# A fused attention and gated feed-forward kernel: x of batch 1 on the GpSimd DMA queue, and another order of the loading phase

## The chip, the core and the metric

The kernel runs on one NeuronCore of a Trainium2 chip. The metric is the device time of one execution in microseconds, as the median of several runs; smaller is better. Five engines work side by side, each through its own list of instructions in order: TensorE (PE in the profile, its weight loads PEld), VectorE (DVE), ScalarE (ACT), GpSimd (POOL) and SyncE (SP), which here only starts DMA transfers. ACT and POOL start transfers too. Transfers that SP starts appear in the profile as queue q1, those of ACT as q10 and those of POOL as q0; all of them are carried by the same 16 DMA engines. Engines wait for each other and for transfers by semaphores.

## What is computed

Eight batches of x (8 heads, 512 tokens, 64 channels) meet a small state (8 heads, 32 rows). Both directions of attention between them are computed, joined to 544 rows of 512 per batch, and put through a feed-forward layer with a sigmoid gate.

```python
scores = scale * np.matmul(x, state.transpose(0, 1, 3, 2))
a = np.exp(scores - scores.max(-1, keepdims=True))
a /= a.sum(-1, keepdims=True) + 1e-09
xread = np.matmul(a, state)
scores2 = scale * np.matmul(state, x.transpose(0, 1, 3, 2))
a2 = np.exp(scores2 - scores2.max(-1, keepdims=True))
a2 /= a2.sum(-1, keepdims=True) + 1e-09
sread = np.matmul(a2, x)
x = np.concatenate([xread, sread], axis=2)   # to (4352, 512)
gate = 1.0 / (1.0 + np.exp(-(x @ w_gate)))
return (gate * (x @ w_val)) @ w_out
```

x, the state and the weights (512 by 1536, 512 by 1536, 1536 by 512) are given as float32, and so is the result.

## The kernel before

The matrix products run in bfloat16. Weights and most of the state are turned into bfloat16 by POOL's transfers themselves; x arrives as float32 (`xf`) and is cast on an engine into `xb` (`cast_x`). A batch then goes through these steps:

- x is transposed to `xT`: for batches 0 and 1 on PE with copies by ACT or DVE (`xT_mm`, `xT_cp`, and `xT_mm2`, `xT_cp2`, two head pairs at a time), for later ones by four transposing transfers on SP (`at_xT_dma`).
- `S_mm` multiplies `xT` with the padded state `sTz`, `S_exp` takes the exponential on ACT. `n_sum`, `n_mul` (or `n_sums`, `n_muls`) on DVE normalise over the state rows into `ab`; `aT_mm` and `aT_cp` (or `aT_dma`) transpose that to `aT`.
- `at_Eb`, `p_tok` and `p_fold` on POOL prepare the other direction, `sr_mm` and `sr_fin` finish it into `XS`, a ninth "batch" that holds the 256 state rows of all batches.
- The attention output isn't formed for the tokens. Instead `sw_visit` (or `sw_wide`) multiplies the state with the weights, and `sw_cp` copies the result to `SW`. For each block f of 128 hidden columns (12 of them), `gv_mm` multiplies `SW` with `aT` and so gives the gate and value projections; `gv_th` (tanh on ACT) and `gv_glu` (DVE) join them into `glu`.
- `out_mm` multiplies four blocks of `glu` with a piece of `wo`; three of these make 128 rows of output, which ACT copies out and SP stores.

PSUM is divided into two banks for `gv`, one for `outp`, four for `swp` and one for `at`; a step names its bank (`GV`, `OU`, `SWP`, `AT`) and waits until what last stood there has been read.

There is no scheduler: the program order of each engine is the order in which the calls are written. From L424 to L673 stands a list of calls, written out one by one, the loading phase. In it x, the weights and the state arrive, batches 0 and 1 are projected, batch 0 is multiplied with `wo`, and batch 2 is prepared. The first call of the loop over b (L675) makes `SW` of batch 3; from there each turn projects batch b, multiplies batch b-1 with `wo` and prepares batch b+1.

Loads of the list, before: SP loads x of batches 0 and 1 in four pieces each (two heads, 256 KB a piece, `load_x(.., 4)`). ACT loads the first quarter of the state (`load_s`), POOL the three others (`load_sb`), the gate and value weights in pieces of 256 or 512 columns (`load_w`; w=0 is `wg`, w=1 is `wv`), `wo` in three pieces (`load_wo`), and x of batches 2 and 3. A POOL transfer is issued by an instruction in POOL's own list and so waits for whatever stands ahead of it. `gate` is a tiny POOL copy out of a tile that a transfer fills: it holds back all that follows on POOL until that has landed. `warm` runs small matmuls on constants, 68 in all.

Of the kernel before, what the change touches and what calls it, by code (L numbers as in the profile page):

```python
# [8 lines left out]
FP = mybir.dt.float32  # L9
BF = mybir.dt.bfloat16  # L10
# [6 lines left out]
def kernel(  # L17
# [14 lines left out]
    nc = tc.nc  # L32
# [55 lines left out]
    def cast_x(b, cp, lo, n):  # L88
        if b not in xbs:
            xbs[b] = xp.tile((128, 4, H, D), BF, name="xb")  # L90
        cp(xbs[b].rearrange("p c h d -> p h c d")[:, lo:lo + n], xfs[b][:, lo:lo + n])  # L91
# [358 lines left out]
    sT_mm(0, SWP)  # L450
    xT_cp(0, 0, vec)
    warm(20, OU)
    cast_x(0, act, 2, 2)
    cast_x(0, vec, 6, 2)
    xT_mm(0, 1, SWP)
    sT_pad(0, 0, vec)
    sT_pad(0, 1, act)
    S_mm(0, 0, SWP, (0,))
    xT_cp(0, 1, vec)
    xT_mm(0, 2, OU)  # L460
    cast_x(1, vec, 2, 2)
    cast_x(1, pool, 0, 2)
    xT_mm(0, 3, GV)
    load_w(1, 1024, 512)
    xT_cp(0, 2, act)
    cast_x(1, pool, 6, 2)
    xT_cp(0, 3, vec)
    cast_x(1, vec, 4, 2)
    load_w(0, 0, 256)
    load_sb(3)  # L470
    S_mm(0, 0, AT, (1,))
    S_exp(0, 0)
    S_mm(0, 1, AT, (0,))
    xT_mm2(1, 0, OU)
    S_mm(0, 1, OU, (1,))
    S_exp(0, 1)
    warm(12, AT)
    xT_cp2(1, 0, act)
    n_sum(0, 0)
    xT_mm2(1, 1, SWP)  # L480
    S_mm(1, 0, GV)
    n_sum(0, 1)
    xT_cp2(1, 1, vec)
    S_mm(1, 1, SWP)
    S_exp(1, 0)
    at_Eb(0)
    sw_visit(0, 256, 256)
    n_mul(0, 0, nc.vector)
    n_mul(0, 1, nc.vector)
    S_exp(1, 1)  # L490
    sT_mm(1, GV)
    sw_cp(0, 256, 2, 1, act)
    p_tok(1)
    n_sums(1)
    sw_cp(0, 256, 2, 0, act)
    aT_mm(0, GV)
    sT_cp(1, act)
    aT_cp(0, 0, act)
    sr_mm(0, AT)
    sw_visit(1, 256, 256)  # L500
    sw_visit(0, 1024, 512, 0)
    aT_cp(0, 1, vec)
    n_muls(1, nc.vector)
    load_sb(2)
    gv_mm(0, 3, GV)
    sw_cp(1, 256, 2, 0, act)
    sw_cp(1, 256, 2, 1, act)
    gv_th(0, 3)
    load_w(1, 0, 256)
    aT_mm(1, OU)  # L510
    sw_cp(0, 1024, 0, 1, act)
    sw_visit(1, 1024, 512, 0)
    sw_cp(0, 1024, 0, 0, vec)
    gv_glu(0, 3)
    sw_cp(1, 1024, 0, 1, act)
    sw_visit(0, 1024, 512, 1)
    sw_cp(1, 1024, 0, 0, vec)
    sw_cp(0, 1024, 1, 0, act)
    sw_visit(1, 1024, 512, 1)
    sw_cp(0, 1024, 1, 1, vec)  # L520
    gv_mm(0, 11, GV)
    aT_cp(1, None, vec)
    sw_cp(1, 1024, 1, 0, act)
    gv_mm(0, 2, SWP)
    sw_cp(1, 1024, 1, 1, act)
    load_w(0, 512, 512)
    gv_th(0, 2)
    gv_th(0, 11)
    gv_mm(1, 2, SWP)
    sr_fin(0)  # L530
    gv_glu(0, 2)
    gv_th(1, 2)
    load_x(2, nc.gpsimd)
    gv_mm(0, 9, SWP)
    gv_glu(0, 11)
    gv_mm(1, 8, GV)
    gv_th(0, 9)
    gv_th(1, 8)
    sT_mm(3, OU)
    gv_glu(1, 2)  # L540
    sw_visit(1, 0, 256)
    gv_glu(0, 9)
    load_w(1, 512, 512)
    sw_visit(0, 0, 256)
    gv_glu(1, 8)
    sw_cp(1, 0, 2, 1, act)
    gv_mm(0, 8, GV)
    sT_mm(2, AT)
    sw_cp(1, 0, 2, 0, act)
    sw_visit(0, 512, 512, 0)  # L550
    sw_cp(0, 0, 2, 0, vec)
    gv_th(0, 8)
    sw_cp(0, 0, 2, 1, vec)
    sT_cp(2, act)
    gv_glu(0, 8)
    sT_cp(3, act)
    sw_visit(1, 512, 512, 0)
    gv_mm(1, 11, GV)
    load_wo(0)
    sw_cp(0, 512, 0, 0, act)  # L560
    sw_cp(0, 512, 0, 1, vec)
    gv_th(1, 11)
    gv_mm(0, 0, SWP)
    gv_glu(1, 11)
    gv_mm(1, 9, GV)
    sw_cp(1, 512, 0, 1, act)
    at_Eb(1)
    sw_cp(1, 512, 0, 0, act)
    gv_th(1, 9)
    gv_th(0, 0)  # L570
    cast_x(2, vec, 4, 4)
    p_fold(1)
    gv_glu(1, 9)
    gv_mm(0, 1, SWP)
    gv_mm(0, 10, GV)
    gv_th(0, 1)
    gv_glu(0, 0)
    gv_th(0, 10)
    sr_mm(1, AT)
    gv_glu(0, 1)  # L580
    gate(xfs[0][:, 7, 0, 0:1])
    cast_x(2, pool, 0, 4)
    sw_visit(0, 512, 512, 1)
    gv_glu(0, 10)
    sw_visit(1, 512, 512, 1)
    sw_cp(0, 512, 1, 0, vec)
    sw_cp(0, 512, 1, 1, act)
    gv_mm(1, 0, GV)
# [8 lines left out]
    gv_glu(1, 0)
    gv_glu(0, 5)
    sr_fin(1)
    gv_mm(0, 6, SWP)  # L600
    gv_mm(0, 7, GV)
    gv_mm(0, 4, SWP)
    gv_th(0, 6)
    gv_th(0, 7)
    out_mm(0, 1, OU)
    gv_glu(0, 6)
    gv_th(0, 4)
    S_mm(2, 1, SWP)
    gv_mm(1, 4, SWP)
    S_mm(2, 0, GV)  # L610
    gv_glu(0, 4)
    gv_glu(0, 7)
    out_mm(0, 7, SWP)
    S_exp(2, 1)
    S_exp(2, 0)
    gv_mm(1, 6, GV)
    gv_th(1, 4)
    gv_th(1, 6)
    out_mm(0, 0, AT)
    gv_glu(1, 6)  # L620
    gv_mm(1, 7, GV)
    gv_glu(1, 4)
# [6 lines left out]
    out_mm(0, 3)
    n_add(2)  # L630
    gv_glu(1, 7)
    n_muls(2, nc.vector)
    out_mm(0, 9)
    at_Eb(2)
    aT_dma(2)
    p_fold(2)
    out_mm(0, 4)
    gv_th(1, 3)
    gv_glu(1, 3)
    out_mm(0, 5)  # L640
    out_mm(0, 11)
    gv_mm(1, 1, GV)
    gv_th(1, 1)
    sw_wide(2, 0)
    out_mm(0, 6, GV)
    gv_glu(1, 1)
    sw_cp(2, 0, 0, 1, act)
    sw_cp(2, 0, 1, 0, act)
    sr_mm(2, GV)
    sw_cp(2, 0, 1, 1, act)  # L650
    sw_cp(2, 0, 2, 1, act)
    sw_cp(2, 0, 0, 0, vec)
    out_mm(0, 8)
    cast_x(3, pool, 0, 4)
    sw_cp(2, 0, 2, 0, act)
    sw_wide(2, 1)
    cast_x(3, act, 4, 4)
    sw_cp(2, 1, 1, 0, act)
    sw_cp(2, 1, 0, 0, act)
    sr_fin(2)  # L660
    at_xT_dma(3)
    sw_cp(2, 1, 1, 1, vec)
    out_mm(0, 10)
    sw_cp(2, 1, 2, 1, vec)
    gv_mm(1, 10, SWP)
    sw_cp(2, 1, 0, 1, vec)
    gv_th(1, 10)
    sw_cp(2, 1, 2, 0, vec)
# [86 lines left out]
```

## Time and profile before

| what | us |
|---|---|
| median of three runs | 226.27 (226.02 to 227.07) |
| span of the profiled execution, first to last instruction | 225.4 |
| own time of the profiled execution | not listed apart from its span |
| PE busy | 216.1 |
| first projection `gv_mm` starts | 16.20 |
| first call of the loop starts on PE | 57.56 |
| x0's four pieces land after their issue (from 0.75 on) | 3.4, 3.6, 4.0, 4.3 |
| `wv` and `wg`, 256 columns, issued and landing after | 4.86 and 6.2; 5.79 and 6.6 |
| `wo` pieces 1 and 2, issued and landing after | 38.25 and 5.8; 39.0 and 8.3 |

The clock that TensorE was granted is 1.0 throughout. The page's slices are a fortieth of the span, 5.6 us each; a digit is the busy share in tenths, and DMA is the mean over 16 engines. In the rows of the timeline the columns are start, duration, engine, line of the code, operation, output and input tile with shapes, and how many; in brackets stands the idle time just before and what ended it. Rows of a DMA queue give packets, megabytes, and the time of the packets as a share of the 16 engines' time in the window.

### The profile page before, as it was taken

Reading aid. Unit: us, or ns where it says so; the run is one execution under the profiler, and the core shown is the slowest. Engines: PE = TensorE matmul, PEld = TensorE weight load, DVE = VectorE, ACT = ScalarE, POOL = GpSimd, SP = SyncE. Lnnn points to the kernel's source line nnn. Section 1 sums busy time; section 2 is a strip of 40 time slices with the busy share of each in tenths; the row PEclk is TensorE's granted clock in tenths of the full one; section 3 lists DMA queues with packets and bytes.
Section 4 is the critical chain, followed back from the end, with each engine's and each line's share of the span. In section 5 each row is a group of like instructions: output and inputs, shape, how many; then the busy total and the mean of one; then the engine's idle time right before and its main releaser. Section 6 shows DMA issues by size and latency. Waiting matters only on the chain.

```text
span 225.4 us, 4817 instructions
## 1 busy us (share of the span) xinstructions
PE 216.1 (96%) x1843; PEld 110.5 (49%) x1843; DVE 132.2 (59%) x228; ACT 128.7 (57%) x242; POOL 77.6 (34%) x164
## 2 busy tenths in 40 slices
PE   7689999899999999999999999999999999999994
PEld 6654444334444444444444444444445444466744
DVE  3799997647658554855585638574766434422301
ACT  3468885339576566757574666656755444433311
POOL 4999832481027502660068005900370000000001
PEclk9999999999999999999999999999999999999999
DMA  6999992995496245614671441236112111111113
GB/s 208 276 204 193 287 157 48 138 261 167 92 292 223 47 93 165 210 35 86 153 245 26 86 126 47 69 70 143 47 61 81 48 47 49 72 69 49 47 33 108
DMA packets 38503, 27.38 MB, mean 121 GB/s; under 512 B 21104, under 2 KB 33776, under 8 KB 38480
## 3 DMA queue, kind: packets, MB, share of 16 engines
q1 hardware_dynamic: 31344, 19.74, 31.2%
q0 software_dynamic: 6848, 7.14, 17.1%
q8 instruction: 14, 0.23, 0.4%
q10 hardware_dynamic: 288, 0.20, 0.4%
q14 instruction: 9, 0.07, 0.1%
HBM read 18.35 MB, written 8.91 MB: 121 GB/s over the span
## 4 chain that ended last, share of the span: by engine, by line
PE 74%; DMA 12%; SPq 4%; POOL 4%; ACT 3%; issue 1%; DVE 1%; POOLq 0%
PE outp L351 34%; PE gvp L320 28%; DMA xf<-in_x_dram 6%; PE gvp L323 5%; SPq L124 4%; DMA wo<-in_moe_w_out_dram 4%; PE swp L268 3%; DMA xT<-xb 2%; PE Sp L132 2%; PE outp L371 1%; ACT SW L306 1%; PE srp L245 1%; POOL sTz L420 1%; SPq L74 1%; ACT E L137 1%
## 5 line engine op out<-in xcount | busy, mean ns | idle before, releaser
L335 DVE SCALAR_TENSOR_TENSOR glu<-th,gvp 128x512 bf16<-128x512 f32 (+1 forms) x108 | 70.0, 656 | 75.9 <-ACT th L330 61.8
L351 PE MATMUL outp<-wo,glu 128*128 128x512 bf16 x396 | 98.5, 379 | 1.2 <-DMA wo<-in_moe_w_out_dram 1.2
L320 PE MATMUL gvp<-aT,SW 128*128 128x512 bf16 x384 | 96.5, 379 | 0.0
L330 ACT ACTIVATE th<-gvp 128x512 f32<-128x512 f32 (+1 forms) x108 | 61.5, 574 | 59.2 <-PE gvp L320 47.1
L320 PEld LDWEIGHTS <-SW 128*128 128x128 bf16 x384 | 36.3, 98 | 45.1 <-issue 3.7
L351 PEld LDWEIGHTS <-glu 128*128 128x128 bf16 x396 | 37.4, 98 | 42.3 <-issue 2.2
L306 ACT CAST SW<-swp 128x512 bf16<-128x512 f32 x73 | 40.5, 588 | 3.9 <-PE swp L268 2.5
L143 POOL CAST Eb<-E 128x256 bf16<-128x256 f32 x32 | 12.0, 427 | 63.1 <-ACT E L137 63.1
L355 ACT ACTIVATE res<-outp 128x512 f32<-128x512 f32 x33 | 19.7, 597 | 19.6 <-PE outp L351 19.5
L362 POOL DMA_DIRECT2D out_dram<-res x2 | 1.1, 532 | 52.4 <-ACT res L355 52.4
L306 DVE CAST SW<-swp 128x512 bf16<-128x512 f32 x23 | 15.2, 681 | 0.0
L91 POOL CAST xb<-xf 128x1024 bf16<-128x1024 f32 (+1 forms) x14 | 12.8, 927 | 3.2 <-DMA xf<-in_x_dram 2.6
L137 ACT ACTIVATE E<-Sp 128x512 f32<-128x512 f32 x16 | 9.6, 602 | 3.4 <-PE Sp L132 3.4
L183 POOL COPY F<-G 32x128 f32<-32x128 f32 x28 | 9.9, 353 | 1.3
L204 DVE TENSOR_TENSOR ab<-E,ri 128x512 bf16<-128x512 f32 x12 | 8.7, 735 | 0.0
L268 PE MATMUL swp<-wg,sTc 64*32 64x512 bf16 (+1 forms) x192 | 8.6, 328 | 0.0
L132 PE MATMUL Sp<-sTz,xT 128*128 128x64 bf16 x128 | 7.0, 193 | 1.6 <-DVE xT L119 0.6
L132 PEld LDWEIGHTS <-xT 128*128 128x128 bf16 x128 | 6.0, 98 | 5.1 <-DVE xT L119 0.7
L178 POOL COPY F<-E 64x128 f32<-64x128 f32 x14 | 4.1, 292 | 12.3 <-DVE E L170 11.8
L150 DVE TENSOR_REDUCE rs<-E 128x16 f32<-128x512 f32 x12 | 8.2, 679 | 0.2 <-ACT E L137 0.2
L268 PEld LDWEIGHTS <-sTc 64*32 64x32 bf16 x384 | 4.5, 91 | 7.6 <-issue 5.4
L250 DVE RECIPROCAL r<-srp 128x128 f32<-128x128 f32 x8 | 7.6, 949 | 0.7 <-PE srp L245 0.7
(75 smaller groups left out, 150.3 us busy)
## 6 DMA issues: line engine op xcount, KB each, us to landing
out_dram<-res SPq DMA_DIRECT2D x31, 256.0 KB, 2.6
xf<-in_x_dram SPq DMA_DIRECT2D x4, 1024.0 KB, 6.3
xf<-in_x_dram SPq DMA_DIRECT2D x8, 256.0 KB, 4.5
xf<-in_x_dram POOLq DMA_DIRECT2D x2, 1024.0 KB, 10.1
wo<-in_moe_w_out_dram POOLq DMA_DIRECT2D x3, 512.0 KB, 8.3
wg<-in_moe_w_gate_dram POOLq DMA_DIRECT2D x2, 512.0 KB, 7.4
wv<-in_moe_w_val_dram POOLq DMA_DIRECT2D x2, 512.0 KB, 9.8
wv<-in_moe_w_val_dram POOLq DMA_DIRECT2D x2, 256.0 KB, 5.5
```

The costliest lines, as they stand in the source:

```text
L91: cp(xbs[b].rearrange("p c h d -> p h c d")[:, lo:lo + n], xfs[b][:, lo:lo + n])
L132: nc.tensor.matmul(ps[:, c, :, jj], xTs[b][:, 2 * i + jj, c], sTz[:, b, 2 * i + jj], start=True, stop=True)
L137: nc.scalar.activation(E1s[b][:, :, :, 2 * i:2 * i + 2].rearrange("p c e j n -> p (c e) j n"), held["S", b, i].rearrange("p c e j n -> p ( ...
L143: nc.gpsimd.tensor_copy(Ebs[b][:, c], E1s[b][:, c])
L268: nc.tensor.matmul(pss[e][j * Ns:(j + 1) * Ns, o:o + n], sTc[rows, b, j] if b > 1 else sTz[rows, b, j, e], (wg, wv)[w][rows, j, lo:lo + n] ...
L306: cp(*sw_left.pop((b, lo, w, e)))
L320: nc.tensor.matmul(ps, SWs[b][:, g, w, fs], aTs[b][:, :, g], start=(g == 0), stop=(g == 1))
L323: nc.tensor.matmul(ps, (wg, wv)[w][:, j, fs], XS[:, j], start=(j == 0), stop=(j == 3))
L330: nc.scalar.activation(th, held["gv", b, f][0], AF.Tanh, scale=0.5)
L335: nc.vector.scalar_tensor_tensor(glus[b][:, f], held["th", b, f], 1.0, held["gv", b, f][1], ALU.add, ALU.mult)
L351: nc.tensor.matmul(ops[b, c], glus[b][:, f, c * 128:(c + 1) * 128], wo[:, f], start=(f == 0), stop=(f == NF - 1))
L355: nc.scalar.activation(res, ops[b, c], AF.Copy, scale=0.5)
```

## The change

The loads of x for batch 1 leave SP. A new function loads some heads of a batch:

```diff
+    def load_xp(b, eng, lo, n):
+        if b not in xfs:
+            xfs[b] = stg.tile((128, H, 4, D), FP, name="xf")
+        v = x[b].rearrange("h (p c) d -> p h c d", c=4)
+        eng.dma_start(xfs[b][:, lo:lo + n], v[:, lo:lo + n])
```

x of batch 0 stays on SP in four pieces, now in the order heads 6 and 7, 2 and 3, 0 and 1, 4 and 5. x of batch 1 is issued by POOL as its first two transfers, heads 4 to 7 and then 0 to 3, ahead of the identity matrix and of all weights. The rest of the list is the same calls in another order, many on another engine or in another bank. The start of the list:

```diff
-    load_s(0, nc.scalar)
-    load_x(0, nc.sync, 4)
-    load_x(1, nc.sync, 4)
-    make_identity(nc, ident)
...
-    cast_x(0, pool, 0, 2)
-    load_w(1, 256, 256)
-    load_w(0, 256, 256)
-    load_sb(1)
-    cast_s(0, vec)
-    cast_x(0, pool, 4, 2)
-    warm(20, SWP)
-    load_w(0, 1024, 512)
-    warm(16, OU)
-    xT_mm(0, 0, OU)
...
+    load_xp(0, nc.sync, 6, 2)
...
+    load_xp(0, nc.sync, 2, 2)
+    load_s(0, nc.scalar)
+    load_xp(1, nc.gpsimd, 4, 4)
+    cast_x(0, act, 2, 2)
+    warm(20, SWP)
+    load_xp(0, nc.sync, 0, 2)
+    warm(20, OU)
+    load_xp(1, nc.gpsimd, 0, 4)
+    make_identity(nc, ident)
+    cast_s(0, vec)
+    nc.vector.memset(sTz, 0.0)
+    cast_x(0, vec, 0, 2)
+    cast_x(0, act, 6, 2)
+    load_w(1, 256, 256)
+    load_w(0, 256, 256)
+    warm(12, GV)
+    xT_mm(0, 1, GV)
+    load_w(0, 1024, 512)
+    load_xp(0, nc.sync, 4, 2)
+    xT_mm(0, 0, AT)
+    load_w(1, 1024, 512)
+    xT_cp(0, 1, act)
+    sT_mm(0, GV)
+    cast_x(0, vec, 4, 2)
+    cast_x(1, pool, 0, 2)
+    xT_mm(0, 2, OU)
+    xT_cp(0, 0, act)
+    xT_mm(0, 3, GV)
...
+    cast_x(1, vec, 6, 2)
+    xT_cp(0, 3, vec)
+    cast_x(1, vec, 4, 2)
...
+    cast_x(1, act, 2, 2)
+    xT_mm2(1, 0, OU)
+    xT_cp2(1, 1, act)
+    xT_cp2(1, 0, act)
...
+    aT_cp(0, 0, act)
...
+    gv_mm(0, 2, GV)
```

Around `wo` and x of batch 2:

```diff
-    gate(xfs[0][:, 7, 0, 0:1])
-    cast_x(2, pool, 0, 4)
...
-    pad(2, 6)
-    at_xT_dma(2)
...
-    gate(xTs[2][:, 0, 3, 0:1]); load_wo(1)
...
-    load_wo(2)
...
-    load_x(3, nc.gpsimd)
...
+    gate(xfs[0][:, 7, 0, 0:1])
...
+    cast_x(2, act, 0, 4)
...
+    load_wo(0)
+    cast_x(2, pool, 4, 4)
...
+    p_fold(1)
...
+    load_wo(1)
...
+    load_wo(2)
...
+    at_xT_dma(2)
...
+    pad(2, 6)
...
+    S_mm(2, 1, OU)
...
+    load_x(3, nc.gpsimd)
...
+    gate(xTs[2][:, 0, 3, 0:1])
+    sw_wide(2, 0)
```

The order of POOL's loads becomes: x1 (two halves), `wv` and `wg` columns 256 to 511, `wg` and `wv` from 1024, `wg` from 0, state piece 1, `wv` from 0, x2, state piece 2, `wv` from 512, state piece 3, `wg` from 512, then `wo` in three pieces and x3. Between them stand POOL's casts and sums of the list.

More of the change, by code (lines that the diff above doesn't have):

```diff
@@ L422 @@
     sbs = {}
-    load_s(0, nc.scalar)
-    load_x(0, nc.sync, 4)
-    load_x(1, nc.sync, 4)
-    make_identity(nc, ident)
+    ident_e = ident.rearrange("p (g e u) -> p e g u", e=2, u=8)
+    load_xp(0, nc.sync, 6, 2)
+    pick = wp.tile((128, 128), BF, name="pick")
+    pre = wp.tile((128, 2), FP, name="pre")
     for e in range(2):
@@ L430 @@
         nc.vector.memset(ones[:, e, 64 - e * 64:128 - e * 64], 0.0)
-    nc.vector.memset(sTz, 0.0)
-    ident_e = ident.rearrange("p (g e u) -> p e g u", e=2, u=8)
-    pick = wp.tile((128, 128), BF, name="pick")
-    nc.gpsimd.memset(pick, 0.0)
+    load_xp(0, nc.sync, 2, 2)
[8 more added lines that the diff above has]
+    cast_s(0, vec)
@@ new lines @@
+    nc.vector.memset(sTz, 0.0)
+    cast_x(0, vec, 0, 2)
[15 more added lines that the diff above has]
+    xT_mm(0, 3, GV)
+    sT_pad(0, 1, act)
+    load_w(0, 0, 256)
+    sT_pad(0, 0, act)
@@ new lines @@
+    S_mm(0, 0, SWP, (0,))
+    S_mm(0, 0, OU, (1,))
+    cast_x(1, vec, 6, 2)
+    xT_cp(0, 3, vec)
+    cast_x(1, vec, 4, 2)
+    xT_cp(0, 2, act)
+    S_mm(0, 1, SWP, (0,))
+    S_mm(0, 1, GV, (1,))
+    S_exp(0, 0)
+    xT_mm2(1, 1, SWP)
+    S_exp(0, 1)
+    cast_x(1, act, 2, 2)
+    xT_mm2(1, 0, OU)
+    xT_cp2(1, 1, act)
+    xT_cp2(1, 0, act)
+    nc.gpsimd.memset(pick, 0.0)
+    n_sum(0, 0)
+    at_Eb(0)
+    n_sum(0, 1)
+    warm(16, SWP)
+    n_mul(0, 0, nc.vector)
+    n_mul(0, 1, nc.vector)
@@ new lines @@
+    S_mm(1, 1, GV)
+    S_exp(1, 1)
+    sw_visit(0, 256, 256)
+    sw_cp(0, 256, 2, 1, act)
+    S_mm(1, 0, AT)
+    aT_mm(0, GV)
+    load_sb(1)
+    sw_cp(0, 256, 2, 0, vec)
+    sw_visit(1, 256, 256)
+    S_exp(1, 0)
+    sr_mm(0, OU)
+    load_w(1, 0, 256)
+    sw_cp(1, 256, 2, 1, act)
+    aT_cp(0, 1, vec)
+    sw_visit(0, 1024, 512, 0)
+    sw_cp(1, 256, 2, 0, act)
+    aT_cp(0, 0, act)
+    sw_cp(0, 1024, 0, 1, act)
+    sw_visit(1, 1024, 512, 0)
+    n_sums(1)
+    sw_cp(1, 1024, 0, 0, act)
@@ new lines @@
+    sw_cp(0, 1024, 0, 0, vec)
+    gv_mm(0, 2, GV)
+    n_muls(1, nc.vector)
+    gv_th(0, 2)
+    sw_cp(1, 1024, 0, 1, act)
+    gv_mm(0, 3, SWP)
+    gv_glu(0, 2)
+    sw_visit(0, 1024, 512, 1)
+    gv_th(0, 3)
+    sw_cp(0, 1024, 1, 0, vec)
+    sw_cp(0, 1024, 1, 1, act)
+    load_x(2, nc.gpsimd)
+    aT_mm(1, AT)
+    gv_glu(0, 3)
+    gv_mm(0, 11, SWP)
+    aT_cp(1, None, vec)
+    gv_th(0, 11)
+    gv_mm(0, 10, GV)
+    gv_glu(0, 11)
+    gv_th(0, 10)
+    gv_mm(0, 9, SWP)
+    gv_glu(0, 10)
@@ new lines @@
+    gv_th(0, 9)
+    gv_mm(1, 2, GV)
+    gv_th(1, 2)
+    gv_glu(0, 9)
+    gv_glu(1, 2)
+    sT_mm(1, AT)
+    sw_visit(1, 1024, 512, 1)
+    sw_visit(0, 0, 256)
+    p_tok(1)
+    sw_cp(1, 1024, 1, 1, act)
+    load_sb(2)
+    gate(xfs[0][:, 7, 0, 0:1])
+    sw_cp(1, 1024, 1, 0, act)
+    gv_mm(0, 8, GV)
+    sw_cp(0, 0, 2, 0, vec)
+    gv_th(0, 8)
+    gv_mm(1, 3, SWP)
+    sw_cp(0, 0, 2, 1, vec)
+    sw_visit(1, 0, 256)
+    gv_th(1, 3)
+    gv_glu(0, 8)
+    gv_glu(1, 3)
+    cast_x(2, act, 0, 4)
@@ new lines @@
+    gv_mm(1, 11, GV)
+    load_w(1, 512, 512)
+    sw_cp(1, 0, 2, 0, act)
+    sw_cp(1, 0, 2, 1, act)
+    gv_mm(0, 1, SWP)
+    gv_mm(1, 9, SWP)
+    at_Eb(1)
+    sr_fin(0)
+    gv_th(0, 1)
+    gv_th(1, 9)
+    load_sb(3)
+    sT_cp(1, act)
+    load_w(0, 512, 512)
+    gv_glu(0, 1)
+    gv_mm(1, 1, SWP)
+    gv_th(1, 11)
+    gv_glu(1, 9)
+    gv_glu(1, 11)
+    gv_th(1, 1)
+    gv_mm(1, 8, SWP)
+    load_wo(0)
+    cast_x(2, pool, 4, 4)
+    gv_mm(0, 0, GV)
+    sT_mm(2, AT)
+    gv_th(1, 8)
@@ L435 @@
+    gv_glu(1, 1)
+    gv_th(0, 0)
+    sT_mm(3, OU)
+    gv_glu(1, 8)
+    sw_visit(0, 512, 512, 1)
+    sw_cp(0, 512, 1, 0, act)
+    sw_visit(0, 512, 512, 0)
+    gv_glu(0, 0)
+    p_fold(1)
+    sT_cp(2, act)
+    sw_cp(0, 512, 0, 0, act)
+    load_wo(1)
+    gv_mm(1, 0, GV)
     for e in range(2):
         nc.gpsimd.memset(pick[e * 64:e * 64 + 64, e * 64:e * 64 + 64], 1.0)
-    pre = wp.tile((128, 2), FP, name="pre")
-    nc.scalar.activation(pre[:, 0:1], ones[:, 0, 0:1], AF.Exp)
-    cast_x(0, pool, 0, 2)
@@ L441 @@
-    load_w(1, 256, 256)
-    load_w(0, 256, 256)
-    load_sb(1)
-    cast_s(0, vec)
-    cast_x(0, pool, 4, 2)
-    warm(20, SWP)
-    load_w(0, 1024, 512)
-    warm(16, OU)
-    xT_mm(0, 0, OU)
[L450 to L580, printed above, removed]
-    gate(xfs[0][:, 7, 0, 0:1])
-    cast_x(2, pool, 0, 4)
[L583 to L588, printed above, removed]
-    pad(2, 6)
-    at_xT_dma(2)
-    sw_cp(1, 512, 1, 1, vec)
-    sw_cp(1, 512, 1, 0, act)
-    gv_mm(0, 5, SWP)
-    gate(xTs[2][:, 0, 3, 0:1]); load_wo(1)
-    gv_th(1, 0)
-    gv_th(0, 5)
@@ L597 @@
[L597 to L622, printed above, removed]
-    gv_th(1, 7)
@@ L624 @@
-    gv_mm(1, 3, SWP)
-    load_wo(2)
-    out_mm(0, 2)
-    n_sums(2)
-    load_x(3, nc.gpsimd)
[L629 to L668, printed above, removed]
+    sw_cp(0, 512, 1, 1, vec)
+    sr_mm(1, AT)
+    load_wo(2)
+    sw_cp(0, 512, 0, 1, vec)
@@ new lines @@
+    gv_th(1, 0)
+    gv_mm(0, 6, SWP)
+    sT_cp(3, act)
+    gv_th(0, 6)
+    at_xT_dma(2)
+    gv_glu(1, 0)
+    gv_glu(0, 6)
+    gv_mm(0, 5, SWP)
+    pad(2, 6)
+    gv_th(0, 5)
+    gv_glu(0, 5)
+    out_mm(0, 1, GV)
+    sw_visit(1, 512, 512, 1)
+    sw_cp(1, 512, 1, 0, vec)
+    sw_visit(1, 512, 512, 0)
+    sw_cp(1, 512, 0, 1, act)
+    out_mm(0, 6, GV)
+    sw_cp(1, 512, 0, 0, act)
+    S_mm(2, 1, OU)
+    sw_cp(1, 512, 1, 1, act)
+    S_mm(2, 0, SWP)
+    S_exp(2, 0)
+    gv_mm(0, 4, SWP)
@@ new lines @@
+    gv_th(0, 4)
+    sr_fin(1)
+    load_x(3, nc.gpsimd)
+    S_exp(2, 1)
+    gv_glu(0, 4)
+    gv_mm(0, 7, SWP)
+    gv_th(0, 7)
+    out_mm(0, 0, AT)
+    n_add(2)
+    gv_glu(0, 7)
+    gv_mm(1, 4, SWP)
+    n_sums(2)
+    n_muls(2, nc.vector)
+    aT_dma(2)
+    gv_th(1, 4)
+    out_mm(0, 2)
+    out_mm(0, 3)
+    gv_glu(1, 4)
+    out_mm(0, 4)
+    gv_mm(1, 6, SWP)
+    p_fold(2)
+    gv_th(1, 6)
+    gv_glu(1, 6)
+    out_mm(0, 5)
+    gate(xTs[2][:, 0, 3, 0:1])
+    sw_wide(2, 0)
+    sw_cp(2, 0, 1, 1, vec)
@@ new lines @@
+    nc.scalar.activation(pre[:, 0:1], ones[:, 0, 0:1], AF.Exp)
+    out_mm(0, 8)
+    cast_x(3, pool, 4, 4)
+    sw_cp(2, 0, 2, 1, act)
+    out_mm(0, 10)
+    out_mm(0, 7, GV)
+    cast_x(3, pool, 0, 4)
+    sw_cp(2, 0, 2, 0, vec)
+    sw_cp(2, 0, 0, 0, act)
+    at_xT_dma(3)
+    sw_cp(2, 0, 1, 0, act)
+    out_mm(0, 9)
+    sw_cp(2, 0, 0, 1, vec)
+    load_x(4, nc.sync)
+    sw_wide(2, 1)
+    sw_cp(2, 1, 1, 1, act)
+    sw_cp(2, 1, 0, 1, vec)
+    sw_cp(2, 1, 2, 1, act)
+    out_mm(0, 11)
+    at_Eb(2)
@@ L669 @@
+    sr_mm(2, GV)
+    sw_cp(2, 1, 0, 0, vec)
+    sw_cp(2, 1, 2, 0, vec)
+    sr_fin(2)
+    gv_mm(1, 10, SWP)
+    sw_cp(2, 1, 1, 0, act)
+    gv_th(1, 10)
+    gv_glu(1, 10)
+    gv_mm(1, 7, SWP)
+    gv_th(1, 7)
     gv_mm(1, 5, GV)
     gv_th(1, 5)
-    gv_glu(1, 10)
-    load_x(4, nc.sync)
+    gv_glu(1, 7)
     gv_glu(1, 5)
```

## The prediction

> **What bounds the kernel now.** Read first: the page's busy rows and slices. The span is 225.4 us and TensorE is busy in 96% of it.
>
> ```profile
> PE 216.1 (96%) x1843; PEld 110.5 (49%) x1843; DVE 132.2 (59%) x228; ACT 128.7 (57%) x242; POOL 77.6 (34%) x164
> ...
> PE   7689999899999999999999999999999999999994
> ...
> PEclk9999999999999999999999999999999999999999
> DMA  6999992995496245614671441236112111111113
> ```
>
> Only the first slices of PE (5.6 us each) have room, and there DMA is full: until about 32 us the 16 engines carry x, then the weights, without a pause. The matmuls of the two orders are the same ones (1843, the 68 warming ones too), and from the loop over b on (L675) the order is untouched and the chain is PE behind PE. So the change is worth what it does to the moment at which PE enters the loop, at 57.56, and that is PE's work before it plus its idle time. Read second: PE's timeline of the stage, for the idle time.
>
> ```profile
> 4.97 0.40 PE L105 MATMUL xTp<-ident,xb 128*128 128x128 bf16 x4 [0.46 <-POOL xb L91]
> ...
> 7.81 0.28 PE L132 MATMUL Sp<-sTz,xT 128*128 128x64 bf16 x4 [0.43 <-ACT sTz L414]
> ...
> 12.70 0.41 PE L132 MATMUL Sp<-sTz,xT 128*128 128x64 bf16 x8 [0.55 <-DVE xT L119]
> ...
> 16.20 1.04 PE L320 MATMUL gvp<-aT,SW 128*128 128x512 bf16 x4
> ...
> 44.13 2.75 PE L351 MATMUL outp<-wo,glu 128*128 128x512 bf16 x12 [0.68 <-DMA wo<-in_moe_w_out_dram]
> 47.42 2.75 PE L351 MATMUL outp<-wo,glu 128*128 128x512 bf16 x12 [0.54 <-DMA wo<-in_moe_w_out_dram]
> ...
> 57.56 0.41 PE L268 MATMUL swp<-wg,sTc 64*32 64x512 bf16 x8
> ```
>
> Three stretches: to 16.20 PE waits through the chain x, transposes, scores, exponentials, normalising, first projection (gv_mm); from 16.20 it is nearly closed; at 44.13 and 47.42 it waits for wo pieces 1 and 2. Four 512-column matmuls start every 0.865 us, so by start times the two waits cost 44.13 - (42.42 + 0.865) = 0.85 and 47.42 - (44.13 + 3 x 0.865) = 0.70 us, the 42.42 being the start of the last projection before.
>
> **The change, part by part.** *wo is no longer held back.* On POOL before, wo pieces 1 and 2 stand behind a gate on the transposed x of batch 2:
>
> ```profile
> 37.80 0.19 POOL L82 CAST pre<-xT 128x1 f32<-128x1 bf16 x1 [7.32 <-DMA xT<-xb]
> 38.25 1.53 POOL L85 DMA_DIRECT2D wo<-in_moe_w_out_dram  x2 [0.27 <-issue]
> ```
>
> They land 5.8 and 8.3 us after their issues, at 44.05 and 47.3. After, piece 1 follows p_fold(1) and piece 2 the two small memsets, and the gate on xT stands later. p_fold(1) waits for the POOL cast of x2 and takes 4.6 us (its rows from 22.12 to 27.0). x2 is now issued about 15 (before: 18.21) and, by the sums of the queue below, lands near 24; the fold ends near 30, and wo comes through at 2.6 us a piece, at about 36 and 38. It is wanted from 42 on. Worth -0.85 - 0.70 = -1.55 us; with the cover of those 4 us gone it is worth nothing.
>
> *The other loads.* Each is costed by the queue: SP's x came at 0.35 MB/us, a weight piece of 256 columns needs 1.35 us of the queue and one of 512 columns 2.6 (landings 11.06, 12.4, 15.7, 18.2 in a row). The bytes ahead of the weights are the same 2.1 MB, so the first pieces still land near 11.1, 12.4, 15.2, 17.9; POOL issues them earlier (from about 2.8 on, not 4.86), which buys nothing, since wv waited 6.2 us for the queue. Four SP issues of 0.45 go, two POOL issues of 0.75 to 0.93 come, behind which only the identity waits (0.55 us, at about 2.3, wanted at 5.5). The state piece 1 moves from 13.7 to about 20, and its transposes move behind eight projections with it. Two POOL casts of x0 and one of x1 go to ACT and DVE (0.62 and 0.47): these lie on the chain below. Exp's tiny activation (0.20) leaves the start; there is one table load either way. At zero: all of that is covered by the wait for x, and costs at most its own 0.2 to 0.6 without it.
>
> *x0 gets a companion: the disputed cost.* Before, x0's four pieces had the hardware queue to themselves and landed at 4.15, 4.9, 5.75 and 6.6 (issue plus 3.4, 3.6, 4.0, 4.3), x1's last at 9.6. After, both halves of x1 are issued by POOL at about 0.74 and 1.5, beside x0's pieces from 0.75 on. If x0 keeps its landings, its last piece (heads 4, 5) is there at 6.6; if the two share to the end, at 9.6, when the 2.1 MB are through. Nothing in the trace shows the two starting together. Two rows bear on it; the first is of 6.4 to 8.3 us, with wv issued at 4.86:
>
> ```profile
> DMA packets 673, 0.65 MB, mean 342 GB/s; under 512 B 39, under 2 KB 673, under 8 KB 673
> q1 hardware_dynamic: 673, 0.65, 106.6%
> ```
>
> No packet of POOL's q0 while SP's q1 had a backlog; with idle engines (wo piece 1: issue 38.25, first packets 39.7) it needs 1.5 us. The second is of 2.6 to 2.8, ACT's state load beside SP's x:
>
> ```profile
> q10 hardware_dynamic: 34, 0.03, 46.4%
> q1 hardware_dynamic: 32, 0.03, 45.8%
> ```
>
> Here two queues that start together share evenly. At 0.74 POOL finds idle engines, so its first half should be in at about 2.3, beside x0's 2.45, and share; its second, issued when the queue is busy, may be late like wv (3.4 us) or not. State 0.13, half of x1 0.52 and two pieces of x0 0.52 MB at 0.365 MB/us end at 5.65; the other two pieces take 1.45 us alone or 2.9 shared; with 0.6 us to the semaphore 7.7 or 9.1. I take 8.3, the middle.
>
> The Trainium skill ("DMA: Bandwidth & Descriptors", Queues, rings and completion order) says that each engine serves its queues in turn, packet by packet. By that rule x0's last piece comes at 9.6 and the sum is the third rival's; the trace agrees for the state load (34 packets against 32) and disagrees for wv (0 of 673).
>
> From that piece to the first projection, by the rows: DVE cast 0.47, transposes and their latency 0.5, then ACT in a row: copy 0.59, two exponentials 0.60, a cast of x1 0.62, two copies of 1.01, two exponentials, three SW casts of 0.54 and the aT copy 0.63, each starting 0.11 before the one before has ended: 6.7 us, with 0.9 of waits on PE between. 8.6 in all: 8.3 + 8.6 = 16.9, against 16.20, +0.7. With 6.6 the ACT row is bound by x1's second half instead and I get 15.8 (-0.4); with 9.6, 18.2 (+2.0).
>
> *The projections after that.* The same work in another order with the same four sw banks. Walking both orders engine by engine with these durations, before's enters the loop at 57.3 (trace: 57.56), and between first projection and loop after's has only small bank waits (0.2 to 0.9 us in single places, as before has), apart from the wo waits. 0, with 0.7 either way.
>
> Sum: +0.7 - 1.55 + 0 = -0.85 us on the span's 225.4: 224.55. The span stands 0.87 under the median of the runs, 226.27, and I keep that distance: 225.4.
>
> **The rivals.**
> 1. *x0 is not delayed*, SP's queue having its way as from 6.4 to 8.3: -0.4 - 1.55 = -1.95, 224.3. Against it: POOL's first half meets idle engines.
> 2. *Forecast*: 225.4; its own range 224.7 to 226.3.
> 3. *x0 shares to the end, or stands behind x1*: +2.0 - 1.55 = +0.45, 226.7; with POOL's queue wholly ahead some 0.4 more.
> 4. *The other side: wo floods the transposes of x2.* The gate that goes kept wo away from four SP transposes. Two that ran beside POOL's loads landed after 4.0 (xT at 29.95, beside wo piece 0) and 4.4 us (aT at 46.89, beside x3); alone 2.4 to 2.6. After, SP starts them at about 28, with a third of wg, then all of wo in flight until 38. If they only land when that backlog is through, the last comes near 41, and S_mm(2,1), which PE reaches at about 38.7 with everything else queued behind it, stands 2.3 us: -0.85 + 2.3 = +1.45, 227.7. It decides once the four need more than 10 us (before: 7.8). For it: the two rows. Against: those lost under 2 us each, and the four are issued 10 us ahead.
>
> **How the numbers follow.** Chances: forecast 0.33, first rival 0.25, third 0.17, fourth 0.25. 0.5%, about what a measurement of this kernel can tell from no change, is 1.13 us: 225.14 and 227.40. Faster: 0.95 of the first and 0.4 of the forecast, 0.37. Slower: 0.9 of the fourth, 0.05 of the forecast and 0.25 of the third, 0.28. Same: the rest, 0.35. The range goes from the first rival less half the bank term (223.9) to the fourth and as much more (228.1).
>
> **What would show it.** Right: no PE wait on wo; x0's last cast on DVE about 8.3 to 8.5; first projection at 16.5 to 17.3; loop entered at 56.4 to 57. First rival: that cast at 6.6. Third: POOL packets as many as SP's from 2.5 on and x0's last cast after 9. Fourth: PE idle on xT before the scores (L132, in the changed kernel L138) at 38 to 41. Wrong altogether if PE waits for weights between 17 and 40, or if the loop, entered earlier, loses it again.

## The result, and the profile after

The changed kernel takes 232.96 us, the median of runs from 231.18 to 235.76, against 226.15 for the kernel before beside it: 1.0264 times as long, 95% interval [1.0216, 1.0312]. Medians are of all runs, while the ratios, here and below, leave out slow runs, those over 1.5% above the fastest of the same kernel (here the one of 235.76). The forecast was 225.4, with a range of 223.9 to 228.1. The profiled execution took 234.35 with a span of 232.6; the span before was 225.4, so 7.2 us more. That is more than the 6.0 us of the ratio: spans stand 1.7 to 1.9 us under their times in all runs of this case, so that the span of 225.4 belongs to an execution of about 227.1, 0.9 above its median, and 234.35 is the longest of the three runs behind the ratio. The page of after, the same rows as before:

```profile
PE 221.2 (95%) x1843; PEld 114.1 (49%) x1843; DVE 131.2 (56%) x225; ACT 131.5 (57%) x247; POOL 77.5 (33%) x164
...
PE   8499999499999999999999999999999999999993
...
PEclk9769999769999999999999999999999999999998
DMA  7999999902786225632563251126112111121113
```

The matmul count is the same, yet PE is busy for 5.1 us longer, and PEclk has fallen twice: in slices 2 and 3 (6 to 17 us) and 8 and 9 (41 to 52 us). Each fall stands beside a hole in PE's row (the 4 of slice 2, the 4 of slice 8). The timeline of PE shows the holes:

```profile
7.99 0.40 PE L111 MATMUL xTp<-ident,xb 128*128 128x128 bf16 x4 [1.39 <-DVE xb L97]
...
10.71 1.03 PE L111 MATMUL xTp<-ident,xb 128*128 128x128 bf16 x8 [2.08 <-DVE xb L97]
...
14.27 1.91 PE L391 MATMUL warm<-ones 128*128 128x128 bf16 x16
...
19.57 1.89 PE L326 MATMUL gvp<-aT,SW 128*128 128x512 bf16 x8
...
42.30 0.20 PE L138 MATMUL Sp<-sTz,xT 128*128 128x64 bf16 x1 [1.43 <-DMA xT<-xb]
44.20 0.87 PE L138 MATMUL Sp<-sTz,xT 128*128 128x64 bf16 x13 [1.70 <-DMA xT<-xb]
44.88 3.60 PE L326 MATMUL gvp<-aT,SW 128*128 128x512 bf16 x8
48.28 1.91 PE L357 MATMUL outp<-wo,glu 128*128 128x512 bf16 x4
...
50.95 2.75 PE L357 MATMUL outp<-wo,glu 128*128 128x512 bf16 x12
...
64.55 0.41 PE L274 MATMUL swp<-wg,sTc 64*32 64x512 bf16 x8
```

PE waits for x0 (through its casts) at 8 and 10.7, the first projection starts at 19.57 instead of 16.20, the scores of batch 2 wait 1.43 + 1.70 us for their transposed x, and the loop is entered at 64.55 instead of 57.56. No projection onto `wo` waits for `wo` any more. Sixteen warming matmuls take 1.91 us at 14.27, and eight projections 3.60 at 44.88, where eight others take 1.89. The windows view says why (engine columns are busy time and count; the third number from the end is the granted clock):

```profile
9.50:16.00 6.50, 5.29 (x57) 5.11 (x58) 5.18 (x10) 4.28 (x7) 4.31 (x10) 0.50 1.31 206
...
16.50:40.00 23.50, 23.42 (x290) 11.22 (x275) 20.87 (x33) 19.42 (x38) 17.22 (x34) 1.00 1.22 190
...
44.00:50.00 6.00, 5.80 (x26) 2.50 (x27) 3.08 (x5) 2.28 (x4) 1.09 (x4) 0.50 0.40 135
```

So the 6.99 us at the loop's entry are made up like this:

- x0's last piece lands at 9.87, not at 8.3. With the forecast's chain of 8.6 us behind it the first projection would stand at 18.47, 2.27 later than before. It stands at 19.57: the other 1.10 are put down to the chain at half clock (e4 below).
- the wait for the transposed x of batch 2: 3.13.
- half clock after it: twelve 512-column matmuls from 44.88 to 49.99 in 5.11 us, at 0.2165 each worth 2.6: 2.5.
- no waits for `wo`: -1.55.

Together 7.45; the rest, -0.46, lies in the order between.

This is the ledger of one execution. The two other runs behind the ratio, 231.57 and 231.18 us, had a mean granted clock of 0.985, the profiled one 0.967. The trace of e2 below, at 0.984, has one stretch of 6.8 us at half clock, this one has two. So half of the time at half clock is probably missing in the others, an estimate from these means; no profile shows which half.

Where does x0 lose its time? The two queues from 5 to 6 us, in after:

```profile
q0 software_dynamic: 66, 0.25, 73.0%
q1 hardware_dynamic: 68, 0.07, 23.1%
```

and in before:

```profile
q1 hardware_dynamic: 360, 0.35, 105.9%
```

The columns are packets, MB and share of the engines' time. POOL's first half of x1, issued at 1.29, sends its first packets between 4.0 and 4.2. From then on the two queues send about equally many packets, but POOL's carry about 4 KB and SP's 1 KB, so POOL moves most of the bytes: from 4 to 6 us q0 has 127 packets with 0.50 MB, q1 240 with 0.23 MB. With that the first half of x1 (0.52 MB) is all but through, and from 6 to 7 SP is nearly alone (333 packets against 17); from 7 to 8 the second half takes its turns (68 packets with 0.28 MB against 114 with 0.11). x0's four pieces land at 4.45, 5.25, 7.5 and 9.87 (before 4.15, 4.9, 5.75, 6.6). And the transposes of x2, in the chain of waits of after:

```profile
33.75 10.40 DMA xT<-xb
```

The last of the four lands 10.4 us after SP issued it; before it took 3.1, and the four 2.5 to 4.0. Between stand `wo` 1 and 2, which POOL issued at 31.51 and 32.63.

### The profile page after: what moved, and what is told of

Read it like the earlier page. It is cut to its first block, busy times and chain, and to the rows that moved or that the text cites. A ratio compares the mean times of both kernels' runs of the same rounds, so it can differ in the third digit from the quotient of the medians.

```text
span 232.6 us, 4812 instructions
## 1 busy us (share of the span) xinstructions
PE 221.2 (95%) x1843; PEld 114.1 (49%) x1843; DVE 131.2 (56%) x225; ACT 131.5 (57%) x247; POOL 77.5 (33%) x164
## 4 chain that ended last, share of the span: by engine, by line
PE 82%; DMA 8%; POOL 5%; SPq 2%; issue 1%; ACT 1%; DVE 0%
PE outp L357 36%; PE gvp L326 31%; PE gvp L329 5%; DMA xT<-xb 4%; PE swp L274 4%; DMA xf<-in_x_dram 3%; PE Sp L138 2%; PE srp L251 1%; PE outp L377 1%; SPq L130 1%; PE xTp L122 1%; PE warm L391 1%; POOL Eb L149 1%; SPq L80 1%; POOL F L189 0%
## 5 line engine op out<-in xcount | busy, mean ns | idle before, releaser
L326 PE MATMUL gvp<-aT,SW 128*128 128x512 bf16 x384 | 98.4, 385 | 0.1
L149 POOL CAST Eb<-E 128x256 bf16<-128x256 f32 x32 | 11.5, 403 | 65.6 <-ACT E L143 65.6
L312 DVE CAST SW<-swp 128x512 bf16<-128x512 f32 x24 | 15.9, 682 | 4.0 <-PE swp L274 4.0
L97 POOL CAST xb<-xf 128x1024 bf16<-128x1024 f32 (+1 forms) x12 | 11.8, 1007 | 3.5 <-DMA xf<-in_x_dram 3.2
L189 POOL COPY F<-G 32x128 f32<-32x128 f32 x28 | 10.7, 383 | 1.3
L391 PE MATMUL warm<-ones 128*128 128x128 bf16 x68 | 7.2, 303 | 1.0 <-DVE ones L436 1.0
```

The costliest lines, as they stand in the source:

```text
L149: nc.gpsimd.tensor_copy(Ebs[b][:, c], E1s[b][:, c])
L189: pool(F[32 * q:32 * q + 32, 1], G[32 * r:32 * r + 32, 0])
L312: cp(*sw_left.pop((b, lo, w, e)))
L326: nc.tensor.matmul(ps, SWs[b][:, g, w, fs], aTs[b][:, :, g], start=(g == 0), stop=(g == 1))
```

## The experiments

The theory after the result: the change takes away two guards. Before, POOL's first transfer stood behind its cast of x0's first piece, and so left the engines to x until x was nearly in; and the gate on the transposed x2 kept `wo` away from the transposes. The rivals: the new order of calls is slower by itself, or the queue that carries x1 matters, not the moment. The expectation stands ahead of each result; ratios are to the kernel before, run beside it.

**e1: x1 back on SP, the rest as changed.**

```diff
-    load_xp(1, nc.gpsimd, 4, 4)
...
-    load_xp(1, nc.gpsimd, 0, 4)
...
+    load_xp(1, nc.sync, 4, 4)    # behind the four pieces of x0
+    load_xp(1, nc.sync, 0, 4)
```

> The changed kernel with both halves of x1 issued by SP behind x0's four pieces; nothing else moved. Theory (three losses: x0 shares the DMA engines with x1 from the start; the transposes of x2 drown behind wo; in both waits TensorE's clock falls to a half): x0's last piece lands near 6.6 instead of 9.9, the clock stays at 1.0 to 20 us, the first projection starts at 16.0 to 16.5 instead of 19.6; the wait for xT of batch 2 stays. 3 to 4 us less than the changed kernel, 227.5 to 229.5. Rival (the queue of x1 does not matter, all is lost at the transposes): no difference beyond 1 us, since the transposes and wo, not x, set the end of the loading phase.

237.94 us, ratio 1.0485 [1.0442, 1.0528]: a miss, and the most useful one. With x1 gone from POOL's list its weights came first, issued from 1.48 on, and fought x instead. The queues from 9 to 10 us:

```profile
q0 software_dynamic: 165, 0.09, 61.6%
q1 hardware_dynamic: 168, 0.17, 61.3%
```

165 packets against 168: two backlogs take turns, one packet each, and so they do from 7 on. (From 5 to 6, just after POOL's start, POOL sends 316 and SP 8; no run explains that microsecond.) x0's last piece is cast at 12.49, x1's second half lands at 17.4 and is transposed at 18.16, as PE's timeline shows, and the first projection comes at 25.52:

```profile
18.16 1.04 PE L122 MATMUL xTp<-ident,xb 128*128 128x128 bf16 x8 [3.48 <-POOL xb L97]
```

So it isn't x1 that must leave POOL's queue; whatever POOL issues early takes part. (The rule of the Trainium skill that the prediction cites, "DMA: Bandwidth & Descriptors", Queues, rings and completion order, agrees with these counts from 9 to 10.)

**e2: `wo` behind the gate again, the rest as changed.**

```diff
-    load_wo(1)
...
-    load_wo(2)
...
     pad(2, 6)
+    gate(xTs[2][:, 0, 3, 0:1])
+    load_wo(1)
+    load_wo(2)
```

> The changed kernel with wo pieces 1 and 2 issued behind a gate on the last transposed x of batch 2, as before the change; x1 stays on POOL. Theory: the wait of 3.1 us on xT before the scores of batch 2 goes and the half clock of 44 to 50.5 us (2.6 us) with it; in their place waits on wo of up to 1.6 us. First projection still at 19.6. 226.5 to 229. Rival (transposes are late because x2 and its cast are late, not because of wo): the wait on xT stays, and wo comes later still: 232 or more.

229.58 us, ratio 1.0122 [1.0087, 1.0157]: 3.4 us less than the changed kernel. PE's timeline:

```profile
40.89 0.63 PE L138 MATMUL Sp<-sTz,xT 128*128 128x64 bf16 x16
...
45.39 1.89 PE L357 MATMUL outp<-wo,glu 128*128 128x512 bf16 x8 [0.42 <-DMA wo<-in_moe_w_out_dram]
...
48.62 1.02 PE L357 MATMUL outp<-wo,glu 128*128 128x512 bf16 x4 [1.34 <-DMA wo<-in_moe_w_out_dram]
```

The scores don't wait; the waits for `wo` are back with 1.76 us. Taking the gate away saved that and cost, in the profiled execution, the stand of 3.13 us and the 2.5 us at half clock.

**e3: both edits, e1 and e2.**

> Both edits: x1 on SP behind x0, wo pieces 1 and 2 held behind the transposed x of batch 2. Theory: the two losses add, so 6 to 8 us less than the changed kernel: 224 to 226.5, that is the kernel before or slightly better. Rival (a third loss in the new order itself): 227.5 or more, with PE waiting in a place that neither edit touches.

235.11 us, ratio 1.0377 [1.0344, 1.041], a miss for e1's reason: first projection at 25.08. That `wo` was held gave 2.8 us against e1, about as in e2.

**e4: e2 with 50 more warming matmuls in the two holes near 7 and 8.5 us.**

```diff
     xT_mm(0, 1, GV)
+    warm(20, SWP)
...
     sT_mm(0, GV)
+    warm(30, SWP)
```

> As with wo held and x1 on POOL, and 50 more warming matmuls on constants put into the two waits for x0 between 6.6 and 10.7 us. Theory: they keep TensorE's clock at 1.0 through 9 to 16 us; the work between 10.7 and 16.4 us (transposes, scores, 16 warming matmuls) then ends about 1.3 us sooner, the first projection starts at 18.0 to 18.6, and the end comes 0.8 to 1.5 us sooner than without them. Rival (ACT and DVE, not TensorE, set that stretch): clock back at 1.0 but the first projection within 0.4 us of 19.6.

228.83 us, ratio 1.0099 [1.0074, 1.0124], clock 1.0 throughout. The first projection starts at 17.69, in e2 at 19.82:

```profile
17.69 1.89 PE L326 MATMUL gvp<-aT,SW 128*128 128x512 bf16 x8
```

x0's last cast starts at 9.32 there, 0.5 sooner than in e2; the other 1.6 us are the clock. Of the 2.1 us, 1.66 are left at the loop's entry and 1.7 in the span of the profiled executions. But e2's profiled execution is the longest of its four, the medians differ by 0.75, and the intervals of the two ratios overlap. So the traces show the clock's price up to the loop; what it costs over many executions isn't settled.

**e5: the kernel before with x1 as two halves on POOL from the start (by the new function `load_xp`), and nothing else.**

```diff
-    load_x(1, nc.sync, 4)
+    load_xp(1, nc.gpsimd, 0, 4)
+    load_xp(1, nc.gpsimd, 4, 4)
```

> The kernel before, with one part of the change alone: x of batch 1 as two halves that POOL issues at the start, ahead of the identity and all weights; order untouched. Theory (a POOL transfer issued near the start takes even turns with x0): x0's last two pieces land at 7.5 to 10 instead of 5.75 and 6.6 as in the changed kernel, the first projection moves from 16.2 to 18.2 to 20 us, loop entry by as much, and the time is 228.5 to 230.5. Rival (the order of the changed kernel makes x late, not the queue): x0 lands by 6.6 as before, first projection within 0.5 us of 16.2, time 226 to 227.

231.11 us, ratio 1.0186 [1.0138, 1.0234]. In before's own order, a hole at the same place and the same late projection, as PE's timeline shows:

```profile
10.74 0.28 PE L138 MATMUL Sp<-sTz,xT 128*128 128x64 bf16 x4 [3.09 <-ACT sTz L420]
...
20.02 1.02 PE L326 MATMUL gvp<-aT,SW 128*128 128x512 bf16 x4
```

DVE's timeline names what the hole waits for:

```profile
9.54 0.43 DVE L97 CAST xb<-xf 128x512 bf16<-128x512 f32 x1 [3.44 <-DMA xf<-in_x_dram]
```

x0's last piece lands at 9.5, before at 6.6, and DVE's half of `sTz`, ahead of ACT's, stands behind its cast. The first projection is 3.8 us late and the time 1.0186 times before's, about 230.5: both at the upper end of what was expected. The clock is 0.50 from 12 to 15. The order isn't needed for this loss; the moving of x1 alone makes it.

**e6: the kernel before with `wo` 1 and 2 issued ahead of the gate, and nothing else.**

```diff
-    gate(xTs[2][:, 0, 3, 0:1]); load_wo(1)
+    load_wo(1); load_wo(2); gate(xTs[2][:, 0, 3, 0:1])
...
-    load_wo(2)
```

> The kernel before, with another part of the change alone: wo pieces 1 and 2 are issued ahead of POOL's gate on the transposed x of batch 2 (the gate stays ahead of x3). Theory (ungated wo holds up the four transposing transfers whatever the order): the last of the four lands 8 to 10.5 us after its issue instead of 2.8, PE stands 1 to 5 us before the scores of batch 2, the two waits for wo (1.55 us) are gone, and with the lower granted clock that follows a stand the time is 227.5 to 231. Rival (the gate cost its 1.55 us and guarded nothing that the order of before needs): 224.7, no PE wait on xT.

231.98 us, ratio 1.0258 [1.0197, 1.032], above the range expected. The stand is larger than in after, 4.56 + 0.23 + 0.23 us, and 3.4 us at half clock follow. PE's timeline:

```profile
42.03 0.20 PE L132 MATMUL Sp<-sTz,xT 128*128 128x64 bf16 x1 [4.56 <-DMA xT<-xb]
...
43.15 1.90 PE L320 MATMUL gvp<-aT,SW 128*128 128x512 bf16 x4
...
50.07 5.34 PE L351 MATMUL outp<-wo,glu 128*128 128x512 bf16 x24
```

The last row is what the ungated `wo` buys: 24 projections in a row without a wait. From 34 to 36 us, while the transposes wait, q1 has 13 packets and q0 299.

**e7: the changed kernel with x1 on SP behind x0, POOL's weights behind a gate on x0's second piece, `wo` held as in e2.**

```diff
-    load_xp(1, nc.gpsimd, 4, 4)
...
-    load_xp(1, nc.gpsimd, 0, 4)
...
+    gate(xfs[0][:, 2, 0, 0:1])    # ahead of load_w(1, 256, 256)
...
+    load_xp(1, nc.sync, 4, 4)     # behind the four pieces of x0
+    load_xp(1, nc.sync, 0, 4)
```

> The changed kernel with x of batch 1 on SP behind x of batch 0, POOL's first weights behind a gate on the second piece of x0 (heads 2 and 3), and wo behind the gate on the transposed x2. Theory (what x lost was the start of POOL's transfers, which before was held by a POOL cast of x0): x0 lands at 4.2 to 6.7, first projection 15.8 to 17, clock 1.0 throughout, wo waits of 1.5 to 2 us remain, time 225 to 227. Rival (the new order is itself slower by what the transfers do not explain): first projection after 18 or time above 228.

227.82 us, ratio 1.0075 [1.0049, 1.0101]: 0.8 above the range. PE's timeline:

```profile
16.01 1.89 PE L326 MATMUL gvp<-aT,SW 128*128 128x512 bf16 x8
...
37.37 0.63 PE L138 MATMUL Sp<-sTz,xT 128*128 128x64 bf16 x16
...
42.67 1.89 PE L357 MATMUL outp<-wo,glu 128*128 128x512 bf16 x8 [1.22 <-DMA wo<-in_moe_w_out_dram]
...
45.87 1.02 PE L357 MATMUL outp<-wo,glu 128*128 128x512 bf16 x4 [1.31 <-DMA wo<-in_moe_w_out_dram]
```

With both guards back the first projection is at 16.01 (before 16.20) and no score waits. What is left are 2.53 us of idle time before the projections onto `wo`, 1.3 more than before (0.68 and 0.54), since this order asks for piece 1 at 41.30, before at 43.28.

**e8: as e7, but x1 as two halves on POOL, behind the same gate.**

> As the run beside it, but x of batch 1 stays on POOL's queue as two halves, issued behind the same gate on the second piece of x0. Theory (the moment of the issue decides, not the queue): x0 lands at 4.2 to 6.8 alone, x1's halves at about 10 and 12, first projection 16.5 to 18, time 225.5 to 228. Rival (x on POOL's queue costs by itself): first projection at 19 or later as in the changed kernel, time above 229.

229.57 us, ratio 1.0135 [1.0105, 1.0164]. x0 lands alone, as in e7. But x1's halves, issued at 5.41 and 6.3, come at 9.5 and 12.3, and its transposes stand ahead of the first projection in PE's list:

```profile
13.35 1.04 PE L122 MATMUL xTp<-ident,xb 128*128 128x128 bf16 x8 [2.10 <-POOL xb L97]
...
19.71 1.89 PE L326 MATMUL gvp<-aT,SW 128*128 128x512 bf16 x8
```

PE's clock falls in this hole too: it is 0.50 from 13.2 to 16.6. The expected landings were right, the projection of 16.5 to 18 was not. So the rival holds as far as this: on POOL x1 either comes early and takes from x0, or comes late itself, for SP had x1's halves in at 7.9 and 9.4 in e7.

**e9: e7 with the gate on the first transposed piece, and `wo` 2 behind the padding.**

```diff
-    pad(2, 6)
-    gate(xTs[2][:, 0, 3, 0:1])
+    gate(xTs[2][:, 0, 0, 0:1])
     load_wo(1)
+    pad(2, 6)
     load_wo(2)
```

> The run with x1 on SP and POOL's weights held, but the gate ahead of wo piece 1 asks for the first of the four transposed pieces of x2 instead of the last, and wo piece 2 follows the padding of batch 2. Theory (the gate need only keep wo off the transposes while their packets run; the last piece lands 2 us after its packets): the gate fires at about 32.5 instead of 36.3, the scores of batch 2 still find their xT, and the wo waits of 1.22 and 1.31 us are mostly gone: 1.5 to 2.5 us off 227.8, so 225.3 to 226.3. Rival (any wo transfer ahead of the last piece holds it up): PE stands over 1 us on xT at 37 to 40 and the time is 227.5 or more.

225.94 us over twelve runs, ratio 0.9982 [0.9959, 1.0005]. The scores still don't wait, piece 1 isn't waited for, piece 2 costs one wait:

```profile
44.46 1.02 PE L357 MATMUL outp<-wo,glu 128*128 128x512 bf16 x4 [1.56 <-DMA wo<-in_moe_w_out_dram]
```

Counted by start times, as the prediction's 1.55, this wait is 1.73 us. With about as much waiting for `wo` as before has, the new order gives before's time.

**e10 and e11: the kernel before, with one index changed.**

```diff
-    gate(xTs[2][:, 0, 3, 0:1]); load_wo(1)
+    gate(xTs[2][:, 0, 0, 0:1]); load_wo(1)    # e10
+    gate(xTs[2][:, 0, 1, 0:1]); load_wo(1)    # e11
```

> The kernel before with one index changed: the gate ahead of wo piece 1 asks for the first transposed piece of x2, not the last. Theory: wo 1 is issued near 34 instead of 38.25, its packets start near 35.8 and its waits (0.85 and 0.70 us) go; the transposes, issued one after another until 35.8, lose at most a little: 224.6 to 225.6. Rival (three transposes behind wo land late as in the run with wo free): PE stands on xT for 2 us or more from 37.3, time 227.5 to 231.

> As the run beside it, but the gate asks for the second transposed piece. Theory: wo 1 is issued near 35, packets from 36.8, when the transposes' packets are all but through; at least 1.2 of the 1.55 us of wo waits go: 224.7 to 225.6, no stand on xT. Rival: two late transposes, PE stands on xT for 1 us or more, time 226.5 or more.

e10: 226.32 us, ratio 0.9994 [0.9971, 1.0016]. Both mechanisms at once: the `wo` waits are gone, and the last transposes are late, as PE's timeline shows:

```profile
39.23 0.32 PE L132 MATMUL Sp<-sTz,xT 128*128 128x64 bf16 x5 [1.68 <-DMA xT<-xb]
```

Three of its twelve runs took 231.6 to 233.2, as long as e6's. e11: 225.23 us (224.88 to 225.99), ratio 0.9966 [0.9947, 0.9984], less than before and after alike. POOL's timeline of e11:

```profile
35.85 0.19 POOL L82 CAST pre<-xT 128x1 f32<-128x1 bf16 x1 [4.85 <-DMA xT<-xb]
36.30 1.54 POOL L85 DMA_DIRECT2D wo<-in_moe_w_out_dram  x2 [0.27 <-issue]
```

and PE's:

```profile
37.37 0.40 PE L132 MATMUL Sp<-sTz,xT 128*128 128x64 bf16 x8
...
43.02 5.34 PE L351 MATMUL outp<-wo,glu 128*128 128x512 bf16 x23
...
55.75 0.41 PE L268 MATMUL swp<-wg,sTc 64*32 64x512 bf16 x8
```

The gate opens 1.95 us sooner than in before, `wo` comes without a wait, the scores don't wait, and the loop is entered at 55.75.

## Why the prediction was wrong

Three steps of the sum failed: the landing of x0's last piece (+0.7 at the first projection, where 2.27 came of it), the clock (no term) and the transposes of x2 (no term in the sum, only a rival).

**`wo` is no longer held back, -1.55: right as to the waits.** After has none for `wo`, and neither has e11. e11's time is 0.8 us under before's, about half of the 1.55, which was read from a longer execution than most. (For the same reason the 0.87 between span and median, which the forecast kept, isn't a distance of one execution; that is about 1.8. It moves the forecast by nothing.)

**The other loads at zero: right for this change, with a wrong reason.** Nothing waited for weights in after. But "wv waited 6.2 us for the queue" was a misreading. `wv` sent nothing for 3.4 us, and so do other POOL transfers that are issued beside SP's x: in after x1, issued at 1.29, needs 2.9 us to its first packets, in e7 `wv`, issued at 5.04, 3.3. By then x was nearly in. e1 shows what an earlier issue of the weights does once x1 no longer stands ahead of them on POOL: the first projection is 6.0 us later than in after, 9.3 later than in before.

**x0's companion, +0.7: the step that failed first, "I take 8.3, the middle".** The landing was 9.87, beyond even the upper bound of 9.6. The prediction has POOL's first half in at 2.3 and lets the queues share the bytes evenly after that; of its 7.7 and 9.1 the middle is, besides, 8.4. The 0 of 673 packets had been taken for a sign that SP's queue may go first; it was the late start. POOL's packets begin at 4.1, not at 2.3, and then the queues share by packets and not by bytes: 66 of POOL's with 0.25 MB against 68 of SP's with 0.07. x1's second half comes at about 9.7, so the two share to the end, as the third rival has it. e5 shows this loss alone.

**The chain of 8.6 us behind it: right at full clock.** In e4, at clock 1.0, it is 17.69 - 9.32 = 8.4; in after 9.7. The prediction had no term for the clock, though it counted idle time of PE. This is the second failed step: a hole has a price behind it too, in the profiled execution 1.1 us at the first and 2.5 at the second.

**The projections after that, 0 with 0.7 either way: right.** The ledger leaves -0.46 there. From the first projection to the loop, without the waits, e11 in before's order takes 39.5 us, e2 and e9 in the new one 38.9.

**The rivals.** "wo floods the transposes of x2" happened as written: the same place, the same wait, 3.13 us instead of 2.3. Its "more than 10 us", counted from the first issue to the last landing (before: 7.8), was 14.35 (29.80 to 44.15). It had a quarter of the chance, held down by two rows of 4.0 and 4.4 us, which had no two `wo` pieces of 512 KB beside them. By size this is the largest failed step: the sum has no term for the transposes, and in the profiled execution they cost 3.13 us of standing and 2.5 of half clock. The third rival happened as well. The failed step behind the range is that the two were weighed against each other: they lie in different stages, nothing in the one keeps the other away, and their costs add. By the prediction's own prices, +2.0 - 1.55 + 2.3, 229.0 would have been the time of both together, outside the range; the clock and the mis-sized landing make the rest.

What remains open: why e10 takes 226 in most runs and 232 in others. Only one of its executions was profiled, and it is of the former kind; nothing shows what differs in the latter.

## What to carry to other kernels

A wait that stands ahead of a transfer's issue may guard another transfer: before moving the issue forward, look which transfers it will then run beside, and try how far the guard can be loosened (here one index, 0.8 us) rather than dropped (here 5.7 us lost). Price a hole in TensorE's work with the slow clock behind it. And rivals that lie in different stages are priced together, not only in turn.

## What the hardware showed

- A POOL transfer that is issued beside SP's x sends its first packets 2.9 (x1 in after), 3.3 (`wv` in e7) or 3.4 us (`wv` in before) after its issue; on idle engines 1.5 (`wo` in before).
- Between two backlogs the engines take turns by packet, whatever the packets hold: 162 to 156, 142 to 143 and 165 to 168 in the microseconds from 7 to 10 in e1, where POOL's carry 0.5 KB and SP's 1 KB; 66 to 68 from 5 to 6 in after and 67 to 71 in e5, where POOL's carry 4 KB. So the queue with the larger packets gets the larger share of the bytes (0.25 MB against 0.07). One microsecond of e1 doesn't fit (5 to 6: 316 to 8).
- Transposing transfers of SP that meet POOL's backlog send far fewer packets than it: 31 against 228 from 34 to 36 in after, 13 against 299 in e6. The last of the four lands 10.4 and 8.9 us after its issue, in before 3.1. Whether loads without a transpose would fare the same there isn't shown.
- TensorE's granted clock halves around holes that needn't be long: in after two of 1.4 and 2.1 us with 0.6 us of work between, and one of 3.1. In e6 it falls at 42.8, 0.8 us after a stand of 4.56 has ended. A stand of 1.68 in e10 leaves it at 1.00. The half clock lasts 3.4 us in e5, e6 and e8, 6.8 in e2 and both times in after, 13.6 in e1: whole multiples of 3.4, though PE is busy for most of it in after. The Trainium skill ("TensorE: Matmul & The Clock Gate", Part 1: The HAM clock gate) says that an idle window of about 3.4 us halves the clock and a busy window of that length restores it. The trace agrees with the length; but the 3.4 us ahead of the two falls in after weren't wholly idle, PE was busy for 1.3 and 1.1 of them.
